# The first two batches' attention output stays in SBUF, and the seven-product stage gets its operands in another order

## The chip, the cores and the metric

The kernel runs on one core of one Trainium2 chip. The metric is device time in microseconds (us) of one execution, the median of several runs; lower is better. All engines work from queues of their own: TensorE (PE, with its weight loads, PEld), VectorE (DVE), ScalarE (ACT), GpSimd (POOL) and SyncE (SP), which here only issues DMAs.

## The reference

Three layers follow one another, in float32. Attention has 4 batches, 12 heads, 448 positions and a head size of 64; it uses a sigmoid in place of a softmax. Its output, 1792 x 768, goes through two feed-forward layers with an inner size of 2048:

```
scores = q @ k.T / 8 - log(448);  attn = sigmoid(scores) @ v      # per batch and head
x  = attn, heads side by side                                     # 1792 x 768
h  = x @ w_in1;   x = (h * sigmoid(h)) @ w_out1                   # first layer
h  = x @ w_in2;   g = (a0 + a1 h + a2 h^2 + a3 h^3) / (1 + |b0||h| + |b1| h^2 + 1e-6)
out = g @ w_out2                                                  # second layer
```

q, k, v are float32; the weights arrive as float64, as bits.

## The kernel before, in words

**Precision.** Most matmuls take operands split into a high part (a ScalarE copy to fp32r) and a low part (a VectorE subtraction of that copy from the source); three passes (high x high, high x low, low x high) make one product. So every operand costs one ScalarE cast and, after it, one VectorE subtraction. `split` does both at once; `split_later` does the cast and leaves the subtraction to the next `flush()`.

**Weights.** `conv()` turns one 128 x 768 piece of float64 weights into float32 by integer work: one ScalarE op (L150), four VectorE ops (L151 to L156), a store to DRAM, and the load of the piece after next. 64 such pieces are spread over the first three stages; what is left when the second matmul of layer 1 begins is spread evenly over its 64 steps.

**Order.** The order on each engine is written out by hand (`tc.manual_schedule()`): it is the order of the calls, and every engine works through its queue in order. Tiles carry the waits; pools opened with `reuse_waits="tile"` may lie where a closed pool lay.

**Stage 1, attention.** 24 head pairs (4 batches x 6), each in two halves, so 48 half steps. A half step multiplies q and k (`attn_QK`, PE L245), applies the sigmoid (ACT L256), transposes a k or q of a later pair (`attn_T`: PE L235 into one spare PSUM bank, read by ACT L237 and then by DVE L238), and multiplies by v (`attn_AV`, PE L263) for the half before. After each pair `attn_E` copies the output from PSUM (DVE L275) and SP stores it to a DRAM tensor xs. A `conv()` stands in every first half up to pair 21.

**Stage 2, first matmul of layer 1**, as seven block products (p1 to p7) in place of eight, for pairs of batches: batches 0 and 1 in groups 0 to 7, batches 2 and 3 in groups 8 to 15. A product is 9 matmuls on PE L416. Its operands are sums and differences of batches (kinds 11, 21, T1 to T4, 22), and sums and differences of weights (s1 to s4 out of one group's `wf` tiles). The order in a group g is p1(g), p2(g), p4(g-1), p6(g), p5(g), p3(g-1), p7(g). `operands0` makes the first set during attention: `load0` reads xs back from DRAM, and one of 21 steps runs in each half from the 26th on. `operands1` and `operands1_late` make the second set during groups 1 to 8, reading xs of batches 2 and 3. `load_w1(g+2)` loads the weights of a group into the `wf` tiles that group g leaves, behind the last read of them (the low part of a22). `sums_12`, `sums_34`, `prep_*` are the weight sums and their splits.

**Stage 3, second matmul of layer 1**, 64 steps `second(n)` of 18 matmuls (PE L552 to L554), each with one operand from DRAM (`load_g`, issued by ACT L518; `split_gd`: ACT L283, DVE L284); in the first 16 steps also a weight piece (`load_wo1`: ACT L533; `split_wo1`: ACT L287, DVE L288). The results p4 and p3 of the last group are worked in between its first steps; `c11` to `c22` apply silu (ACT L435) to the four quarters of a group's result, `keep` and `both` (ACT L490, DVE L305) gather them from PSUM.

**Stage 4, layer 2**, is not touched.

Of the kernel before, what the change touches and what calls it, by code (L numbers as in the profile page):

```python
# [11 lines left out]
F32 = mybir.dt.float32  # L12
F32R = mybir.dt.float32r
# [28 lines left out]
def attention_moe_moe(ctx: ExitStack, tc: tile.TileContext, q, k, v, w_in1, w_out1, w_in2, w_out2, a, b2, out):  # L42
# [23 lines left out]
    def fixed(nm, n, shape, dt, pool=cpool):  # L66
        return [pool.tile(shape, dt, tag=f"{nm}{i}", name=f"{nm}{i}") for i in range(n)]
# [147 lines left out]
    ijH, ijL, s12H, s12L = fixed("wr", 4, [P, DM], F32R, w1_p)  # L215
    s3H, s3L, s4H, s4L, a22H, a22L = fixed("wq", 6, [P, HM], F32R, w1_p)
# [55 lines left out]
    def attn_E(i):  # L272
        b, hp = divmod(i, NP)
        t = xio.get()
# [3 lines left out]
        del vs[i]  # L278
# [51 lines left out]
    sets = ((wf[1][0], wf[1][1], s34f), (wf[0][0], wf[0][1], s12f))  # L330

    def load0(kk):
        x, y, z = (t[:, :S] for t in sets[kk % 2])
        load_b(x, 0, 0, kk, 0)
        load_b(y, 0, 0, kk, 1)
        load_b(z, 0, 1, kk, 1)

    def operands0():
        for kk in range(HK):
            x, y, z = (t[:, :S] for t in sets[kk % 2])  # L340
# [5 lines left out]
            sub(y, z, y)  # L346
            split_b(y, 0, "T3", kk)
            load_b(y, 0, 1, kk, 0)
            yield
            split_b(z, 0, "22", kk)  # L350
            yield
            sub(x, z, x)
            split_b(x, 0, "T2", kk)
            yield
            split_b(y, 0, "21", kk)
            yield
            sub(y, y, x)
            split_b(y, 0, "T4", kk)
            yield
# [3 lines left out]
    def operands1():  # L363
        y, z, y2 = (t[:, :S] for t in xio.free)
        for kk in range(HK):
            x, w = kept["T1", kk], kept["T2", kk]
            load_b(x, 1, 0, kk, 0)
            load_b(y, 1, 0, kk, 1)
            load_b(z, 1, 1, kk, 1)
            load_b(y2, 1, 1, kk, 0)  # L370
            split_b(x, 1, "11", kk)
            yield
            sub(x, y, x)
            split_b(y2, 1, "21", kk)
            yield
            sub(w, z, x)
            yield

    def operands1_late(kind):
        temps = [t[:, :S] for t in xio.free]  # L380
        if kind == "T2":
            for kk in range(HK):
                load_b(temps[kk], 1, 0, kk, 1)
        if kind in ("T2", "T1"):
            for kk in range(HK):
                split_b(kept[kind, kk], 1, kind, kk)
        if kind == "T1":
            for kk in range(HK):
                load_b(kept["T1", kk], 1, 1, kk, 1)
        if kind == "T3":  # L390
            for kk in range(HK):
                sub(temps[kk], kept["T1", kk], temps[kk])
                split_b(temps[kk], 1, kind, kk)
            for kk in range(HK):
                load_b(temps[kk], 1, 1, kk, 0)
        if kind == "22":
            for kk in range(HK):
                split_b(kept["T1", kk], 1, kind, kk)
        if kind == "T4":
            for kk in range(HK):  # L400
                sub(temps[kk], temps[kk], kept["T2", kk])
                split_b(temps[kk], 1, kind, kk)
# [36 lines left out]
    def prep_ij(g):  # L439
        if g < NGR:  # L440
            split_later(wf[g % 2][0], ijH, ijL)
# [7 lines left out]
    def prep_s12(g):  # L449
        if g < NGR:  # L450
            split_later(s12f, s12H, s12L)
# [6 lines left out]
    def prep_s3(g):  # L458
        split_later(s34f[:, :HM], s3H, s3L)

    def prep_s4(g):
        split_later(s34f[:, HM:], s4H, s4L)

    def prep_a22(g):
        split_later(wf[g % 2][1][:, HM:], a22H, a22L)

    def p1(g):
        product(g, "11", bank("a", g), ijH, ijL, 0, True)

    def p2(g):  # L470
        product(g, "21", bank("b", g), ijH, ijL, HM, True)

    def p3(g):
        product(g, "22", bank("c", g), s4H, s4L, 0, False)

    def p4(g):
        product(g, "T4", bank("a", g), a22H, a22L, 0, False)

    def p5(g):
        product(g, "T1", bank("c", g), s12H, s12L, 0, True)  # L480

    def p6(g):
        product(g, "T2", bank("a", g), s12H, s12L, HM, False)

    def p7(g):
        product(g, "T3", bank("a", g), s3H, s3L, 0, False)
# [249 lines left out]
    with tc.manual_schedule():  # L736
# [36 lines left out]
        for i in range(NPT):  # L773
            for h in range(2):
# [21 lines left out]
                if at_half == -6:  # L796
                    load_w1(0)
                flush()
                if i == NPT - 2 and h == 1:
                    prep_ij(0)  # L800
                    sums_12(0)
                if i == NPT - 1:
                    if h == 0:
                        prep_s12(0)
                    else:
                        prep_a22(0)
                if h == 0 and 0 < i < NPT - 2:
                    conv()
# [5 lines left out]
        load_w1(1)  # L814
# [16 lines left out]
        last = NGR - 1  # L831
        for g in range(NGR):
            was = g >= 1
            fill = 1 <= g < HF - 1
# [7 lines left out]
            if g == HF:  # L842
                operands1_late("22")
# [28 lines left out]
            prep_ij(g + 1)  # L872
            if g == HF:
                operands1_late("T4")
# [6 lines left out]
            keep(g, "r")  # L881
            if g:
                prep_a22(g)
            if g == HF - 1:
                operands1_late("T3")
            if fill:
                next(ops1, None)
# [9 lines left out]
            sums_12(g + 1)  # L897
# [21 lines left out]
        c12(last - 1)  # L919
        p4(last)  # L920
# [112 lines left out]
```

## Time and profile before

| | us |
|---|---|
| median of 3 runs (lowest, highest) | 1144.32 (1143.12, 1149.67) |
| the profiled execution | 1145.94 |
| its span, first to last instruction | 1144.2 |
| PE busy in it | 1100.3 (96%) |
| DVE, ACT, POOL busy | 865.0, 633.0, 341.8 |

A wait is listed by the engine that waits, the line of the instruction, and what came last of what it waited for. "xio", "xa", "xb", "wf", "wr", "wq" are tiles, with numbers left out; "km", "qm" are k and q in the order in which they are transposed. PEclk is the granted TensorE clock as a share of full speed.

### The profile page before, as it was taken

To read this page: it belongs to the slowest core of one execution; us is meant where nothing else is said; L and a number is where in the kernel's file an instruction comes from. 1 tells how busy PE (TensorE), PEld (TensorE's weight loads), DVE (VectorE), ACT (ScalarE), POOL (GpSimd) and SP (SyncE) were. 2 spreads that over 40 slices of the span, in tenths; PEclk is the share of its full clock that TensorE was granted. 3 is DMA by queue.
4 is the path that set the end of the run, shared out by engine and by line. 5 is a ranking of instruction groups with operands and counts; after the bars stand their busy time and mean duration, and the time that the engine had idled before them with its cause. 6 is when DMAs were issued, how large, how long until landed. Compare 5 with 4: busy or idle time off the path is not lost.

```text
span 1144.2 us, 15865 instructions
## 1 busy us (share of the span) xinstructions
PE 1100.3 (96%) x5822; PEld 917.0 (80%) x5822; DVE 865.0 (76%) x1028; ACT 633.0 (55%) x1035; POOL 341.8 (30%) x246
## 2 busy tenths in 40 slices
PE   9999989989989979899999899999999999999997
PEld 5554445979889968799999888888999888889997
DVE  4666776758787736866665849789999988788996
ACT  6777767536655534432322436455766665466664
POOL 2111110000000000000000127556677666556774
PEclk9999999989999999999999999999999999999999
DMA  9999975555757757788888655000101010001001
GB/s 254 294 293 309 276 246 178 194 189 185 241 167 230 246 191 235 263 280 289 276 273 294 234 213 222 1 28 15 56 1 47 10 42 1 21 22 56 1 1 42
DMA packets 103805, 183.47 MB, mean 160 GB/s; under 512 B 8752, under 2 KB 77872, under 8 KB 103728
## 3 DMA queue, kind: packets, MB, share of 16 engines
q1 hardware_dynamic: 91504, 160.89, 43.9%
q10 hardware_dynamic: 12160, 21.57, 5.6%
q8 instruction: 46, 0.75, 0.3%
q14 instruction: 31, 0.25, 0.1%
q0 software_dynamic: 64, 0.00, 0.0%
HBM read 126.06 MB, written 56.36 MB: 159 GB/s over the span
## 4 chain that ended last, share of the span: by engine, by line
PE 77%; DMA 9%; DVE 7%; ACT 3%; issue 2%; SPq 1%; ACTq 1%; POOL 0%; DVEq 0%; POOLq 0%
PE acc L683 14%; PE acc L416 9%; PE acc L686 7%; PE hb L614 7%; PE hb L613 7%; PE hb L612 7%; PE hb L263 5%; PE pair L245 4%; PE acc L553 3%; PE acc L554 3%; PE acc L552 3%; PE hb L416 3%; DMA f<-gd 2%; PE hb L235 2%; PE hb L554 1%
## 5 line engine op out<-in xcount | busy, mean ns | idle before, releaser
L288 POOL TENSOR_TENSOR w<-wif,w 128x768 fp32r<-128x768 f32 x33 | 61.7, 1869 | 489.5 <-ACT w L287 484.6
L256 ACT ACTIVATE f<-pair,nls 112x896 f32<-112x896 f32 x96 | 96.7, 1012 | 18.3 <-PE pair L245 18.2
L553 PE MATMUL acc<-xa,woH 128*128 128x448 f32 x252 | 93.2, 370 | 3.1 <-DVE xa L284 3.1
L552 PE MATMUL acc<-xa,woH 128*128 128x448 f32 x252 | 93.0, 369 | 0.0
L554 PE MATMUL acc<-xa,woL 128*128 128x448 f32 x252 | 92.8, 368 | 0.0
L263 PE MATMUL hb<-f,vs 112*64 112x448 f32 x384 | 85.2, 567 | 0.0
L640 DVE RECIPROCAL stg<-stg 128x512 f32<-128x512 f32 (+1 forms) x28 | 84.9, 3032 | 0.0
L627 ACT ACTIVATE stg<-hb,absb 128x512 f32<-128x512 f32 (+1 forms) x44 | 28.0, 636 | 98.0 <-PE hb L614 97.9
L150 ACT ACTIVATE bits<-stg 128x768 f32<-128x768 f32 x64 | 58.0, 906 | 41.7 <-DMA stg<-in_moe_w_in_dram 18.0
L245 PEld LDWEIGHTS pair<-xa,xa 64*112 64x112 f32 x576 | 47.9, 176 | 40.1 <-issue 33.8
L283 ACT CAST xa<-f 128x448 fp32r<-128x448 f32 x64 | 35.9, 563 | 75.8 <-DMA f<-gd 57.2
L245 PE MATMUL pair<-xa,xa 64*112 64x448 f32 x576 | 72.9, 385 | 0.0
L416 PE MATMUL acc<-xb,wr 128*128 128x448 f32 x315 | 69.0, 370 | 0.2 <-ACT f L490 0.2
L288 POOL TENSOR_TENSOR wh<-wif,wh 128x768 fp32r<-128x768 f32 x31 | 57.4, 1851 | 26.7 <-DVE xio L632 23.9
L416 PEld LDWEIGHTS acc<-xb,wr 128*128 128x128 f32 x315 | 60.2, 191 | 6.1 <-issue 0.7
L156 DVE SCALAR_TENSOR_TENSOR bits<-stg,bits 128x768 int32<-128x768 int32 x64 | 63.1, 986 | 2.2
L153 DVE SCALAR_TENSOR_TENSOR bits<-stg,bits 128x768 int32<-128x768 int32 x64 | 62.9, 983 | 2.2
L683 PE MATMUL acc<-w,hx 128*128 128x512 f32 x174 | 61.4, 394 | 0.0
L151 DVE TENSOR_SCALAR bits<-bits 128x768 f32<-128x768 f32 x64 | 36.1, 564 | 32.8 <-ACT bits L150 32.4
L683 PE MATMUL acc<-wh,hx 128*128 128x512 f32 x171 | 60.3, 393 | 0.0
L288 POOL TENSOR_TENSOR w<-wof,w 128x768 fp32r<-128x768 f32 x32 | 59.2, 1849 | 0.4 <-ACT w L287 0.3
L288 POOL TENSOR_TENSOR wh<-wof,wh 128x768 fp32r<-128x768 f32 x32 | 59.2, 1851 | 0.1
(197 smaller groups left out, 3170.6 us busy)
## 6 DMA issues: line engine op xcount, KB each, us to landing
stg<-in_moe_w_in_dram SPq DMA_DIRECT2D x32, 768.0 KB, 6.9
stg<-in_moe_w_out_dram SPq DMA_DIRECT2D x32, 768.0 KB, 5.6
gd<-f SPq DMA_DIRECT2D x64, 224.0 KB, 3.3
f<-gd ACTq DMA_DIRECT2D x64, 224.0 KB, 4.6
wf<-w0i SPq DMA_DIRECT2D x32, 384.0 KB, 5.9
w0i<-bits SPq DMA_DIRECT2D x16, 384.0 KB, 4.1
w0o<-bits SPq DMA_DIRECT2D x16, 384.0 KB, 2.6
wos<-w0o ACTq DMA_DIRECT2D x16, 384.0 KB, 4.7
```

The source lines that it names most:

```text
L245: nc.tensor.matmul(p[:CP, j, :S], K[rows[j], a_, c * CP : (c + 1) * CP], Q[rows[j], b_, :], start=(n == 0), stop=(n == 2),)
L256: nc.scalar.activation(t[:CP], p[:CP, :, :S], AF.Sigmoid, bias=nls[:CP], scale=QKSCALE)
L263: nc.tensor.matmul(pav[0][j * D : (j + 1) * D, :S], vs[i][:, j, c * D : (c + 1) * D], t[:CP, j], start=(c == 0), stop=(c == NCH - 1),)
L288: (eng or nc.vector).tensor_tensor(out=lo, in0=src, in1=h.bitcast(F32), op=ALU.subtract)
L416: nc.tensor.matmul(o, w_[:, w], x[:, i_, :], start=first and kk == 0 and n_ == 0, stop=kk == HK - 1 and n_ == 2, skip_group_check=not first,)
L552: nc.tensor.matmul(o, woH[c][:, w], x[:, 0, :], start=(c == 0), stop=False)
L553: nc.tensor.matmul(o, woH[c][:, w], x[:, 1, :], start=False, stop=False)
L554: nc.tensor.matmul(o, woL[c][:, w], x[:, 0, :], start=False, stop=(c == KF - 1))
L612: nc.tensor.matmul(o, wh[:, w], x[:, 0, :wd_], start=first, stop=False)
L613: nc.tensor.matmul(o, wh[:, w], x[:, 1, :wd_], start=False, stop=False)
L640: nc.vector.reciprocal(t0, t1)
L683: nc.tensor.matmul(acc[t][:, :BK], a_, w_[:, :BK], start=first, stop=last)
```

## The change

Four things are changed. (1) `attn_E` leaves the output of batches 0 and 1 in twelve SBUF tiles `xk`, stores nothing to DRAM for them, and `operands0` works on these tiles; its steps start four halves earlier, and each subtraction now stands behind the split of the step, for the next step to use. The `xk` tiles lie where the split weights `wr`, `wq` lie later. (2) The last `conv()` in attention is that of pair 18, `load_w1(0)` and `load_w1(1)` come eight halves before the end, the first weight splits from five halves before the end. (3) In stage 2 `operands1` issues its loads a step or more before it splits them; T3 and T4 are subtracted for all three tiles some products before they are split; `sums_12` moves from behind p3 to behind p4, `prep_s3` from behind p4 to behind p6, `prep_ij` from behind p6 to behind p5; a `conv()` stands in groups 0, 2, 4, 6 and 10 to 15 (before: 9 to 15). (4) At the end of stage 2 the last group's c21, the gathering of its r and c12 move behind the third step of stage 3. The order on PE and on POOL is the same as before.

```
+    xk = fixed("xk", 2 * KD, [P, S], F32, xk_p)
     def attn_E(i):
+        if b < 2:
+            nc.vector.tensor_copy(xk[b * KD + hp], pav[0][:, :S])
+            return
     def operands0():
         for kk in range(HK):
-            x, y, z = (t[:, :S] for t in sets[kk % 2])
+            x, w, y, z = (xk[kk + n_ * HK] for n_ in range(4))
             split_b(x, 0, "11", kk)
+            sub(x, y, x)
             yield
-            sub(x, y, x)
             split_b(x, 0, "T1", kk)
+            sub(y, z, y)
             yield
...
     def operands1():
+        load(0)
+        yield
         for kk in range(HK):
-            load_b(x, 1, 0, kk, 0)
...
             split_b(x, 1, "11", kk)
             yield
+            split_b(y2, 1, "21", kk)
             sub(x, y, x)
-            split_b(y2, 1, "21", kk)
             yield
             sub(w, z, x)
+            if kk + 1 < HK:
+                load(kk + 1)
+                yield
             yield
...
-                if at_half >= -NOPS - 2:
+                if at_half >= -NOPS - 6:
                     next(first_ops, None)
-                for kk, when in enumerate((-NOPS - 5, -NOPS - 4, -NOPS + 6 + 1)):
-                    if at_half == when:
-                        load0(kk)
...
-                if h == 0 and 0 < i < NPT - 2:
+                if h == 0 and 0 < i < NPT - 5:
                     conv()
...
             both(g, "s1", "b")
-            prep_s3(g)
-            if g == HF - 1:
-                operands1_late("T1")
-            if fill:
-                next(ops1, None)
-            if g in (0, 2, 4, 6) or g > HF:
+            sums_12(g + 1)
+            if was:
+                fill(g)
+            if g in (0, 2, 4, 6) or g > HF + 1:
                 conv()
...
         p4(last)
-        both(last, "u3", "c")
         c22(last)
         second(1)
-        c21(last)
         p3(last)
-        both(last, "r", "c")
-        c12(last)
...
             second(n)
+            if n == 2:
+                c21(last)
+                both(last, "r", "c")
+                c12(last)
```

VectorE in attention, one head pair (pair 15; hb0 is the spare bank, hb1 the output; xa are split k and q, xb the operands). Before:

```order
L238 TENSOR_TENSOR xa4_220<-hb0_276,xa4_220 128x448
L302 TENSOR_TENSOR wf1_1_252<-wf1_1_252,wf1_0_251 128x448
L284 TENSOR_TENSOR xb6_234<-wf1_1_252,xb6_234 128x448
L238 TENSOR_TENSOR xa5_221<-hb0_276,xa5_221 128x448
L275 COPY xio0_61<-hb1_277 128x448
L284 TENSOR_TENSOR xb1_229<-wf0_0_249,xb1_229 128x448
L151 TENSOR_SCALAR bits0_66<-bits0_66 128x768
L152 TENSOR_SCALAR bits0_66<-bits0_66 128x768
L153 SCALAR_TENSOR_TENSOR bits0_66<-stg1_65,bits0_66 128x768
L156 SCALAR_TENSOR_TENSOR bits0_66<-stg1_65,bits0_66 128x768
L238 TENSOR_TENSOR xa0_216<-hb0_276,xa0_216 128x448
```

and in the changed kernel, the densest kind of pair:

```order
L239 TENSOR_TENSOR xa2_218<-hb0_281,xa2_218 128x448
L288 TENSOR_TENSOR xb13_241<-xk1_259,xb13_241 128x448
L306 TENSOR_TENSOR xk7_265<-xk10_268,xk7_265 128x448
L239 TENSOR_TENSOR xa3_219<-hb0_281,xa3_219 128x448
L280 COPY xio2_63<-hb1_282 128x448
L288 TENSOR_TENSOR xa7_223<-xk7_265,xa7_223 128x448
L306 TENSOR_TENSOR xk7_265<-xk10_268,xk1_259 128x448
L151 TENSOR_SCALAR bits2_68<-bits2_68 128x768
L152 TENSOR_SCALAR bits2_68<-bits2_68 128x768
L153 SCALAR_TENSOR_TENSOR bits2_68<-stg0_64,bits2_68 128x768
L156 SCALAR_TENSOR_TENSOR bits2_68<-stg0_64,bits2_68 128x768
L239 TENSOR_TENSOR xa4_220<-hb0_281,xa4_220 128x448
```

The subtraction (L302, now L306) has moved behind the split that it stood ahead of.

VectorE in group 0 of stage 2, from the weight sums s3, s4 (sf1) to the low part of s3 (wq1). Before:

```order
L302 TENSOR_TENSOR sf1_254<-wf0_0_249,wf0_1_250 128x384
L302 TENSOR_TENSOR sf1_254<-wf0_0_249,sf0_253 128x384
L305 TENSOR_TENSOR f_60<-acc2_1994,f_60 128x448
L151 TENSOR_SCALAR bits0_66<-bits0_66 128x768
L152 TENSOR_SCALAR bits0_66<-bits0_66 128x768
L153 SCALAR_TENSOR_TENSOR bits0_66<-stg1_65,bits0_66 128x768
L156 SCALAR_TENSOR_TENSOR bits0_66<-stg1_65,bits0_66 128x768
L298 TENSOR_TENSOR wq1_260<-sf1_254,wq0_259 128x384
```

and in the changed kernel:

```order
L306 TENSOR_TENSOR sf1_254<-wf0_0_249,wf0_1_250 128x384
L306 TENSOR_TENSOR sf1_254<-wf0_0_249,sf0_253 128x384
L309 TENSOR_TENSOR f_60<-acc2_1968,f_60 128x448
L309 TENSOR_TENSOR sf0_253<-wf1_1_252 128x384
L306 TENSOR_TENSOR sf0_253<-sf0_253,wf1_0_251 128x384
L151 TENSOR_SCALAR bits0_66<-bits0_66 128x768
L152 TENSOR_SCALAR bits0_66<-bits0_66 128x768
L153 SCALAR_TENSOR_TENSOR bits0_66<-stg0_64,bits0_66 128x768
L156 SCALAR_TENSOR_TENSOR bits0_66<-stg0_64,bits0_66 128x768
L302 TENSOR_TENSOR wq1_1844<-sf1_254,wq0_1843 128x384
```

The two sums of the next group (sf0 out of wf1) now stand ahead of the conversion and of wq1.

ScalarE at the change from stage 2 to stage 3 (acc0 is the last group's result, gd the DRAM operands, woH the split weights). Before:

```order
L435 ACTIVATE f_60<-f_60 128x448 x2
L435 ACTIVATE f_60<-acc0_1992 128x448
L435 ACTIVATE f_60<-f_60 128x448
L287 CAST woH2_3693<-wos2_3497 128x768
L533 DMA wos2_3497<-w0o6_158 128x768
L283 CAST xa2_218<-f_60 128x448
L518 DMA f_60<-gd4_0_97 128x448
L283 CAST xa3_219<-f_60 128x448
```

and in the changed kernel:

```order
L442 ACTIVATE f_60<-f_60 128x448 x2
L291 CAST woH2_3656<-wos2_3464 128x768
L540 DMA wos2_3464<-w0o6_158 128x768
L287 CAST xa2_218<-f_60 128x448
L525 DMA f_60<-gd4_0_97 128x448
L442 ACTIVATE f_60<-acc0_1966 128x448
L442 ACTIVATE f_60<-f_60 128x448
L287 CAST xa3_219<-f_60 128x448
```

The two silus of the last group now stand behind the operands of step 2 and ahead of those of step 3.

## Rows read from the trace of the kernel before

**Rows 1.** Windows, two stages: us, busy of PE, PEld, DVE, ACT, POOL; PEclk; DMA share, GB/s.

```profile
88.40:195.10 106.70, 95.17 (x606) 47.11 (x605) 77.55 (x117) 79.09 (x109) 15.00 (x20) 0.97 0.82 253
195.10:409.90 214.80, 205.05 (x991) 187.81 (x991) 159.65 (x265) 118.92 (x219) 0.00 (x0) 0.98 0.64 212
```

**Rows 2.** Waits of PE: line, releaser, us in total, times, longest.

```profile
PE hb L235 <- DVE xa L238: 11.5, 8, 2.1
PE acc L416 <- ACT f L490: 8.5, 3, 5.4
...
PE hb L416 <- ACT f L490: 1.0, 1, 1.0
PE acc L416 <- DVE wq L298: 0.3, 1, 0.3
```

**Rows 3.** Chain of waits, attention and stage 2: start, us, what.

```profile
12.82 1.66 PE hb L263 x8
...
88.42 1.68 PE hb L263 x8
...
182.74 1.65 PE hb L263 x8
...
228.22 6.67 DMA T<-xs
...
239.51 8.51 PE acc L416 x27
...
273.82 12.77 PE acc L416 x63
```

**Rows 4.** Timeline of DVE, attention without operand steps: start, us, what.

```profile
69.13 0.56 DVE L151 TENSOR_SCALAR bits<-bits 128x768 f32<-128x768 f32 x1
...
72.19 0.61 DVE L238 TENSOR_TENSOR xa<-hb,xa 128x448 fp32r<-128x448 f32 x1
```

**Rows 5.** Timeline of PE, the transpose that follows.

```profile
73.42 0.60 PE L235 MATMUL hb<-ident,qm 112*128 112x112 f32 x4
```

**Rows 6.** Timeline of DVE, attention with operand steps.

```profile
107.13 0.93 DVE L151 TENSOR_SCALAR bits<-bits 128x768 f32<-128x768 f32 x1 [0.19 <-ACT bits L150]
...
139.54 0.61 DVE L275 COPY xio<-hb 128x448 f32<-128x448 f32 x1
140.07 0.61 DVE L302 TENSOR_TENSOR wf<-sf,wf 128x448 f32<-128x448 f32 x1
```

**Rows 7.** Timeline of POOL, its copy at the first of these.

```profile
107.03 0.61 POOL L193 COPY km<-ks 112x512 f32<-112x512 f32 x1 [9.05 <-DMA ks<-in_k_dram]
```

**Rows 8.** Timeline of ACT, the last of the three T4 casts in stage 2.

```profile
317.54 0.56 ACT L283 CAST xb<-xio 128x448 fp32r<-128x448 f32 x1 [1.23 <-DVE xio L302]
```

**Rows 9.** Timeline of DVE, stage 2: a low part, a weight sum.

```profile
203.11 0.95 DVE L298 TENSOR_TENSOR wr<-wf,wr 128x768 fp32r<-128x768 f32 x1
203.98 0.55 DVE L305 TENSOR_TENSOR sf<-wf 128x384 f32<-128x384 f32 x1
```

**Rows 10.** Tile wf, groups 10 to 15: landing of its loads.

```profile
DMA to landing us min/median/max: 5.9/6.5/7.7
```

**Rows 11.** Timeline of DVE, stage 3: low parts of three weight pieces.

```profile
452.85 0.96 DVE L288 TENSOR_TENSOR woL<-wos,woH 128x768 fp32r<-128x768 f32 x1
...
458.73 0.95 DVE L288 TENSOR_TENSOR woL<-wos,woH 128x768 fp32r<-128x768 f32 x1
...
461.96 0.96 DVE L288 TENSOR_TENSOR woL<-wos,woH 128x768 fp32r<-128x768 f32 x1
```

**Rows 12.** Timeline of ACT, the operand of step 3.

```profile
428.85 0.56 ACT L283 CAST xa<-f 128x448 fp32r<-128x448 f32 x1
```

**Rows 13.** Timeline of PE, first matmuls of step 2.

```profile
428.98 0.47 PE L552 MATMUL hb<-xa,woH 128*128 128x448 f32 x1 [4.00 <-ACT xa L283]
...
430.34 0.57 PE L552 MATMUL hb<-xa,woH 128*128 128x448 f32 x1
430.71 0.57 PE L553 MATMUL hb<-xa,woH 128*128 128x448 f32 x1
```

More of the change, by code (lines that the diff above doesn't have):

```diff
@@ L328, in split_b @@
         split(src, x)
-    sets = ((wf[1][0], wf[1][1], s34f), (wf[0][0], wf[0][1], s12f))
-    def load0(kk):
-        x, y, z = (t[:, :S] for t in sets[kk % 2])
-        load_b(x, 0, 0, kk, 0)
-        load_b(y, 0, 0, kk, 1)
-        load_b(z, 0, 1, kk, 1)
     def operands0():
         for kk in range(HK):
-            x, y, z = (t[:, :S] for t in sets[kk % 2])
+            x, w, y, z = (xk[kk + n_ * HK] for n_ in range(4))
             split_b(x, 0, "11", kk)
+            sub(x, y, x)
             yield
-            sub(x, y, x)
             split_b(x, 0, "T1", kk)
+            sub(y, z, y)
             yield
-            sub(y, z, y)
             split_b(y, 0, "T3", kk)
-            load_b(y, 0, 1, kk, 0)
+            sub(y, z, x)
             yield
@@ L364, in operands1, with load @@
         y, z, y2 = (t[:, :S] for t in xio.free)
-        for kk in range(HK):
-            x, w = kept["T1", kk], kept["T2", kk]
-            load_b(x, 1, 0, kk, 0)
+        def load(kk):
+            load_b(kept["T1", kk], 1, 0, kk, 0)
             load_b(y, 1, 0, kk, 1)
@@ L370, in operands1 @@
             load_b(y2, 1, 1, kk, 0)
+        load(0)
+        yield
+        for kk in range(HK):
+            x, w = kept["T1", kk], kept["T2", kk]
             split_b(x, 1, "11", kk)
             yield
+            split_b(y2, 1, "21", kk)
             sub(x, y, x)
-            split_b(y2, 1, "21", kk)
             yield
             sub(w, z, x)
+            if kk + 1 < HK:
+                load(kk + 1)
+                yield
             yield
@@ L389, in operands1_late @@
                 load_b(kept["T1", kk], 1, 1, kk, 1)
+        if kind == "T3 sums":
+            for kk in range(HK):
+                sub(temps[kk], kept["T1", kk], temps[kk])
         if kind == "T3":
             for kk in range(HK):
-                sub(temps[kk], kept["T1", kk], temps[kk])
                 split_b(temps[kk], 1, kind, kk)
@@ L398, in operands1_late @@
                 split_b(kept["T1", kk], 1, kind, kk)
+        if kind == "T4 sums":
+            for kk in range(HK):
+                sub(temps[kk], temps[kk], kept["T2", kk])
         if kind == "T4":
             for kk in range(HK):
-                sub(temps[kk], temps[kk], kept["T2", kk])
                 split_b(temps[kk], 1, kind, kk)
@@ L450, in prep_s12 @@
         if g < NGR:
-            split_later(s12f, s12H, s12L)
+            split_later(s12f, wr[2], wr[3])
     def sums_34(g):
@@ L790, in attention_moe_moe @@
                 at_half = 2 * i + h - 2 * NPT
-                if at_half >= -NOPS - 2:
+                if at_half >= -NOPS - 6:
                     next(first_ops, None)
-                for kk, when in enumerate((-NOPS - 5, -NOPS - 4, -NOPS + 6 + 1)):
-                    if at_half == when:
-                        load0(kk)
-                if at_half == -6:
+                flush()
+                if at_half == -8:
                     load_w1(0)
-                flush()
-                if i == NPT - 2 and h == 1:
+                    load_w1(1)
+                if at_half == -5:
+                    xk_s.close()
+                    wr_p, wr_s = opened("wr")
+                    wr.extend(fixed("wr", 4, [P, DM], F32R, wr_p))
+                    wq.extend(fixed("wq", 6, [P, HM], F32R, wr_p))
                     prep_ij(0)
                     sums_12(0)
[L802 to L806, printed above, removed]
-                if h == 0 and 0 < i < NPT - 2:
+                if at_half == -3:
+                    prep_s12(0)
+                if at_half == -1:
+                    prep_a22(0)
+                if h == 0 and 0 < i < NPT - 5:
                     conv()
@@ L831, in attention_moe_moe, with fill @@
         last = NGR - 1
+        def fill(g):
+            if g < HF - 1:
+                next(ops1, None)
         for g in range(NGR):
             was = g >= 1
-            fill = 1 <= g < HF - 1
             p1(g)
@@ L842, in attention_moe_moe @@
             if g == HF:
+                operands1_late("T3")
+            if g == HF + 1:
                 operands1_late("22")
@@ L871, in attention_moe_moe @@
                 c21(g - 1)
-            prep_ij(g + 1)
+            prep_s3(g)
+            if g == HF - 1:
+                operands1_late("T1")
             if g == HF:
-                operands1_late("T4")
+                operands1_late("T4 sums")
             if g == last:
@@ L881, in attention_moe_moe @@
             keep(g, "r")
+            prep_ij(g + 1)
             if g:
                 prep_a22(g)
[L884 to L887, printed above, removed]
+            fill(g)
+            if g == HF:
+                operands1_late("T4")
             if g == last:
@@ L896, in attention_moe_moe @@
             load_w1(g + 2)
-            sums_12(g + 1)
+            if g == HF - 1:
+                operands1_late("T3 sums")
             if g == last - 1:
@@ L919, in attention_moe_moe @@
         c12(last - 1)
+        both(last, "u3", "c")
         p4(last)
-        both(last, "u3", "c")
         c22(last)
         second(1)
-        c21(last)
         p3(last)
-        both(last, "r", "c")
-        c12(last)
+        wr_s.close()
         w1_s.close()
```

38 lines of the change are left out of this document (18 added, 20 removed).

## The prediction

> **What bounds the kernel now.** I read the windows by stage first: the reader is to see that PE is busy for 95.17 of the 106.70 us of the later attention and 205.05 of the 214.80 us of stage 2 [rows 1]. PE bounds the kernel, so only time that PE stands still, or runs at its lower clock, can be won. The waits of PE come second: 11.5 us for DVE's reading of the transposed q and k, in eight waits, and 8.5 + 1.0 + 0.3 us in stage 2, most of it for one ScalarE copy out of PSUM that is late [rows 2]. The chain of waits comes third and tells how much is lost in all.
>
> In attention the half steps come every 3.60 us up to 88.42 ((88.42 - 12.82) / 21 steps); the next 22 steps should take 79.2 us and take 94.3 [rows 3]. So 15.1 us are lost there: the 11.5 us of waits, and 3.6 us behind them, in part at a lower clock. The loss begins where the operand steps do. DVE shows why, by its order: a period holds the copy of the output, two splits, one or two subtractions, a conversion and two readings of the transposes, and a split whose source was only just subtracted waits for ACT's cast in between.
>
> In stage 2 the longest wait of PE, 5.4 us, ends at 239.51. Ahead of it the chain shows a load of xs of 6.67 us [rows 3]: ACT, in order, stands at the cast of a tile whose load was only just issued, and the copy that PE waits for is queued behind. Then 27 matmuls take 8.51 us, where 63 undisturbed ones take 12.77, or 0.203 each [rows 3]: 8.51 - 5.47 = 3.0 us more, at the lower clock. The other waits, 8.5 - 5.4 + 1.0 = 4.1 us, stand at groups 7 and 8, where a cast waits 1.23 us for the subtraction ahead of it [rows 8], three times in T3 and three times in T4, with a copy for PE queued behind. So stage 2 loses 5.4 + 3.0 + 4.1 + 0.3 = 12.8 us.
>
> **Attention.** Twelve stores and twelve loads leave SP's queue, and with them 5.5 MB. SP no longer holds q, k, v loads behind loads that wait for stores. Nothing is added to DVE: the copy goes to another tile, splits and subtractions are as many as before. What moves is their order, so the waits for casts go. What is late next is DVE itself. Without operand steps its reading of a transposed k ends at 72.19 + 0.61 = 72.80, and PE takes up the spare bank at 73.42 [rows 4, 5]: 0.62 us to spare. In the first half of a pair a split and, in most, a subtraction now stand between the output copy and the conversion, 0.53 us each (139.54 to 140.07) [rows 6]. A split alone fits; with a subtraction it is 1.06 - 0.62 = 0.44 us too late. Eight pairs (11 to 18) have both operand steps and a conversion, and by the order five of them the subtraction: 2.2 us. POOL adds to it: while its copy of k ran at 107.03, a conversion op took 0.93 us in place of 0.56 [rows 4, 6, 7], 0.37 more. Once in each of the five pairs that are late is 1.9 us. I take 4.0 us lost, so 11.1 won. The bounds: nothing lost (15.1 won), and in all eight pairs the 0.44 and two such collisions, 8 x 1.18 = 9.4 lost (5.7 won).
>
> The Trainium skill ("SBUF — State Buffer", section "SBUF: two separate sides") says that DVE and GpSimd share a port pair as an exclusive lock, held for a whole instruction, and that a DVE op with two SBUF inputs takes it too. That speaks against this change, which packs such subtractions where POOL's copies fall. The 0.93 us agrees that the two get in each other's way; by the rule a collision would cost up to one whole POOL copy, 0.61 us.
>
> The three conversions that leave (3.06 us of DVE each, 69.13 to 72.19 [rows 4]) stood in pairs 19 to 21; those pairs then have DVE to spare. The four early weight loads and first splits stand behind the last operand step; the `xk` tiles that the splits overwrite have been read by then, so I cost this at nothing.
>
> **Stage 2.** With a load issued half a group (6 us) or more ahead of its cast, against 6.67 us for the slowest shown, the 5.4 us and the 3.0 at low clock go; the second and third loads have a whole group, 12.8 us. With the three subtractions ahead of all three casts the 4.1 us go. SP may now wait for a subtraction before such a load, with stores and the load of a conversion behind it, and none of these is needed within a group.
>
> Two costs come. In group 0 PE waited 0.3 us at p7 for the low part of s3, which stands behind a conversion; now two sums, 0.55 us each [rows 9], stand ahead of it too: 0.3 + 1.1 = 1.4 us. And `sums_12` now stands three products earlier, 5.5 us, while the load it reads is still issued behind the low part of a22. From that low part round to the next one: the load 6.5 us [rows 10], two sums 1.1, a conversion 3.06, the low parts of s3, ij and a22, 0.55 + 0.87 + 0.55 (203.11 to 203.98 for the long one [rows 9]), together 12.6 us, against 12.77 for a group. It just fits; at 7.7 us it is 1.1 us late per group with a conversion. I take 0.5 us in all, bounds 0 and 6 x 1.1 = 6.6 (groups 10 to 15). So stage 2 wins 12.8 - 1.4 - 0.5 = 10.9 us, bounds 4.8 and 11.4.
>
> **Stage 3.** Before, step 2's operands stood behind c12, which waits for the last p3: PE waited 4.00 us, from 424.98 to 428.98, and about ten matmuls ran at 0.37 us each instead of 0.203 [rows 13], 1.7 us more. These 5.7 us go at that point. But I expect them back. From step 3 on, a chain through ACT and DVE sets the pace: a step without a conversion takes 461.96 - 458.73 = 3.2 us, one with it 458.73 - 452.85 = 5.9 [rows 11], against 18 x 0.203 = 3.65 on PE. Step 3's cast stood at 428.85, 3.9 us behind p3's end [rows 12, 13]; now it stands behind both and c12, and so begins 0.6 + 0.5 us behind it, 2.8 earlier. PE comes 5.7 earlier. And as 36 conversions are left in place of 32, eight and not seven fall into steps 3 to 15: 5.9 - 3.2 = 2.7 us more. Won: 2.8 - 2.7 = 0.1 us; bounds -5 (the load latencies of this stretch once more) and +5.7. One cast of s3 now stands just ahead of the operands of step 0: 0.4 us lost. The other conversions lie beside steps where PE had no lasting wait: nothing, with the bound of -5 covering it.
>
> **Sum.** 11.1 + 10.9 + 0.1 - 0.4 = 21.7 us. The profiled execution took 1145.94, so 1124.2; the median of the runs lies 1.6 us below it, so 1122.6.
>
> **Rivals.**
> - *DVE stays the bound of attention.* 5.7 won there in place of 11.1: 1128.0. For it: DVE is as full as before. Against it: the waits for casts, which were part of each period, go. Chance 0.17. By the Trainium skill's rule on the shared pair ("SBUF — State Buffer"), as an estimate, 0.61 us for each of two copies in each of eight pairs, 9.8 us, would bring the time out here too.
> - *Conversion pace.* The four conversions that moved into stage 3 take 2.7 us each from PE, one in the sum already: 8.1 more, 1130.7. For it: the chain of rows 11; against it: from step 16 on no weight pieces stand in the chain. Chance 0.15.
> - *The sums meet their loads* (slower). In the ten groups with a conversion DVE waits for the load at `sums_12`, and p7 and p1 wait for low parts behind it. It decides from 21.7 / 10 + 6.6 = 8.8 us of landing on; at 9.5 us it costs 10 x 2.9 = 29 us: 1151.6. Against it: the slowest shown is 7.7. Chance 0.04.
> - *The change does not do what it says*: the stalls only move to the next load or cast, and just one of the two stages gains, some 11 us: 1133. Chance 0.07.
> - *Better*: no collisions, and stage 3 keeps its 5.7: 15.1 + 11.4 + 5.7 - 0.4 = 31.8 won, 1112.5. Nothing in DVE's order excludes it. Chance 0.10.
>
> The forecast itself has 0.47; its own range is 1117 to 1128. The range for 8 in 10 is 1112 to 1133. Half a per cent, 5.7 us, is about what a measurement of this kernel can tell from no change: faster than that 0.93, within it 0.03, slower 0.04.
>
> **What would show it.** Right: attention ends near 184 (before: 195.1), the waits of PE for DVE's reading of the transposes fall to some 3 us in few pieces; no wait over 2 us in stage 2, one of about 1.4 at the first p7, and no stretch of 0.37 us matmuls there; stage 2 lasts about 204; step 2 of stage 3 follows p3 at once, and more waits for low parts of weights come in steps 5 to 15. Wrong: DVE waiting at `sums_12` for a load in group after group, or PE still waiting two microseconds at every transposition of q.

## The result, and the profile after

The changed kernel takes 1132.43 us (median of 4 runs, 1128.91 to 1134.14), the kernel before 1145.09 beside it: ratio 0.988, 95% interval 0.984 to 0.992. The forecast was 1122.6 with a range of 1112 to 1133, so the time lies just inside the range and 10 us above its centre. The profiled execution took 1133.58 us, against 1145.94 before: 12.4 us won.

Windows of the changed kernel: later attention, stage 2, and stage 3 from step 2 to step 63 (columns as in [rows 1], which answer to the first two).

```profile
87.96:182.39 94.43, 91.74 (x605) 46.20 (x605) 66.59 (x104) 77.54 (x105) 14.16 (x19) 1.00 0.73 222
182.39:387.13 204.74, 201.95 (x992) 185.31 (x991) 154.28 (x259) 119.43 (x218) 0.00 (x0) 1.00 0.63 212
403.12:654.97 251.85, 234.12 (x1100) 207.54 (x1099) 167.31 (x234) 81.93 (x128) 4.61 (x2) 0.99 0.79 261
```

The kernel before, steps 2 to 63:

```profile
428.98:667.36 238.38, 230.75 (x1098) 206.98 (x1099) 155.82 (x218) 78.12 (x123) 4.33 (x2) 0.99 0.77 257
```

The reader is to see two things. Attention ends at 182.39 in place of 195.10, and stage 2 takes 204.74 in place of 214.80: at step 0 of stage 3 the change is 409.90 - 387.13 = 22.8 us ahead. But steps 2 to 63 take 13.5 us more than before, with PE standing 251.85 - 234.12 = 17.7 us there in place of 7.6. (DVE works 11.5 us more: four conversions.) The lead by step: 25.9 us at step 2, 22.2 at step 16, 19.7 at steps 32 and 48, 12.4 at step 63, and nothing changes after that.

The waits of PE in the changed kernel (columns as in [rows 2]):

```profile
PE acc L560 <- DVE xa L288: 6.1, 8, 2.4
PE hb L560 <- DVE xa L288: 4.7, 5, 1.3
PE acc L559 <- ACT xa L287: 3.5, 1, 3.5
PE hb L559 <- DVE f L309: 2.8, 1, 2.8
PE hb L236 <- DVE xa L239: 2.7, 5, 0.6
PE hb L561 <- DVE woL L292: 1.9, 5, 0.4
PE hb L559 <- ACT woH L291: 1.7, 1, 1.7
PE acc L423 <- DVE wq L302: 1.5, 2, 1.3
...
PE hb L423 <- DVE wq L302: 1.3, 1, 1.3
```

Of [rows 2], the 11.5 us for transposes are 2.7 us in five pieces, and the 8.5 us for ScalarE's copy are gone. What stands at the top now are operands and weight pieces of stage 3 (L559 to L561). In stage 2 two waits of 1.3 remain, and DVE's timeline there shows, at the sums that groups 11 to 14 make for the next group, what answers to [rows 9, 10]:

```profile
327.53 0.56 DVE L309 TENSOR_TENSOR sf<-wf 128x384 f32<-128x384 f32 x1 [2.09 <-DMA wf<-w0i]
...
340.72 0.56 DVE L309 TENSOR_TENSOR sf<-wf 128x384 f32<-128x384 f32 x1 [2.40 <-DMA wf<-w0i]
...
355.05 0.56 DVE L309 TENSOR_TENSOR sf<-wf 128x384 f32<-128x384 f32 x1 [3.54 <-DMA wf<-w0i]
...
368.11 0.56 DVE L309 TENSOR_TENSOR sf<-wf 128x384 f32<-128x384 f32 x1 [2.26 <-DMA wf<-w0i]
```

The sums do meet their loads, but of each 2 to 3.5 us only the longest reaches PE (1.30 at 359.78).

The timeline of ACT, around steps 50 to 55, is the place of the longest wait in stage 3:

```profile
602.45 0.55 ACT L287 CAST xa<-f 128x448 fp32r<-128x448 f32 x1
607.48 0.91 ACT L150 ACTIVATE bits<-stg 128x768 f32<-128x768 f32 x1 [4.48 <-DMA wif<-w1i]
613.96 0.62 ACT L603 CAST hx<-xio 128x512 fp32r<-128x512 f32 x1 [5.58 <-DMA xio<-xs]
613.97 0.34 ACTq L525 DMA_DIRECT2D f<-gd  x1
614.49 0.56 ACT L287 CAST xa<-f 128x448 fp32r<-128x448 f32 x1
```

Between 602.45 and 614.49 ACT casts no operand for PE: it stands at a conversion and at the cast of layer 2's x, and PE waits 3.53 us at 615.10. Before the change ACT had lead enough to hide such stands (the account below gives it at step 48).

### The profile page after: what moved, and what is told of

It is laid out like the page before. It is cut to its first block, busy times and chain, and to the rows that moved or that the text cites. A ratio compares the mean times of both kernels' runs of the same rounds, so it can differ in the third digit from the quotient of the medians.

```text
span 1131.8 us, 15809 instructions
## 1 busy us (share of the span) xinstructions
PE 1096.3 (97%) x5822; PEld 913.8 (81%) x5822; DVE 862.2 (76%) x1028; ACT 636.3 (56%) x1035; POOL 341.8 (30%) x246
## 4 chain that ended last, share of the span: by engine, by line
PE 80%; DVE 8%; DMA 7%; ACT 2%; issue 2%; ACTq 1%; SPq 0%; POOL 0%; DVEq 0%; POOLq 0%
PE acc L690 14%; PE acc L423 10%; PE acc L693 7%; PE hb L621 7%; PE hb L619 7%; PE hb L620 7%; PE hb L264 6%; PE pair L246 5%; PE hb L423 4%; PE acc L560 3%; PE acc L561 3%; PE acc L559 3%; DMA f<-gd 3%; PE hb L236 2%; DVE bits L153 1%
## 5 line engine op out<-in xcount | busy, mean ns | idle before, releaser
L559 PE MATMUL acc<-xa,woH 128*128 128x448 f32 x252 | 93.9, 372 | 3.6 <-ACT xa L287 3.5
L561 PE MATMUL acc<-xa,woL 128*128 128x448 f32 x252 | 93.4, 371 | 0.0
L264 PE MATMUL hb<-f,vs 112*64 112x448 f32 x384 | 82.5, 551 | 0.0
L423 PE MATMUL acc<-xb,wr 128*128 128x448 f32 x315 | 67.8, 366 | 0.0
L423 PEld LDWEIGHTS acc<-xb,wr 128*128 128x128 f32 x315 | 59.0, 188 | 5.5 <-issue 0.7
L288 DVE TENSOR_TENSOR xa<-f,xa 128x448 fp32r<-128x448 f32 x64 | 39.0, 620 | 30.1 <-ACT xa L287 30.1
```

The source lines that it names most:

```text
L264: nc.tensor.matmul(pav[0][j * D : (j + 1) * D, :S], vs[i][:, j, c * D : (c + 1) * D], t[:CP, j], start=(c == 0), stop=(c == NCH - 1),)
L423: nc.tensor.matmul(o, w_[:, w], x[:, i_, :], start=first and kk == 0 and n_ == 0, stop=kk == HK - 1 and n_ == 2, skip_group_check=not first,)
L559: nc.tensor.matmul(o, woH[c][:, w], x[:, 0, :], start=(c == 0), stop=False)
L561: nc.tensor.matmul(o, woL[c][:, w], x[:, 0, :], start=False, stop=(c == KF - 1))
```

## The experiments

**e1: conversions put back.** The four that moved into stage 3 go back to attention (three) and stage 2 (one).

```
-                if h == 0 and 0 < i < NPT - 5:
+                if h == 0 and 0 < i < NPT - 2:
-            if g in (0, 2, 4, 6) or g > HF + 1:
+            if g in (0, 2, 4, 6) or g > HF:
```

> The changed kernel with the four conversions put back where they were (pairs 19 to 21 of attention, group 9 of stage 2), so that 32 and not 36 are left for stage 3. Theory 'conversion pace' (the four extra conversions set the pace of stage 3 and cost about 10 us there): steps 2 to 63 of stage 3, which take 238.4 us in the kernel before and 251.9 in the changed one, take 238 to 243; attention and stage 2 lose 0 to 2 us; the whole is 1120 to 1125. Rival 'latency' (stage 3 got slower because its loads and stores now fall otherwise, whatever the number of conversions): steps 2 to 63 still take 249 to 253 and the whole is 1131 to 1135.

Measured: 1124.01 us, ratio 0.981 (0.979 to 0.983). Steps 2 to 63, windows:

```profile
408.76:645.87 237.11, 228.24 (x1100) 207.20 (x1099) 155.54 (x218) 78.62 (x124) 3.96 (x2) 0.99 0.77 257
```

So with the four, stage 3 takes 251.85 - 237.11 = 14.7 us more. Some 2 us of this are another thing, a slower pace of PE's matmuls in the changed kernel (see e7): 28 of its 61 steps lasted 3.72 us, and none of e1's, where an undisturbed step lasts 3.65. Step 0 comes 5.5 us later than in the changed kernel (attention 1.8, the rest in stage 2), where 0 to 2 were expected. That is no clean price of the old places: in e6, which is the changed kernel up to there, step 0 comes 3.9 us later too, and e8 and e10, which differ in the four alone, have it within 0.8 us of each other.

**e2: the kernel before, with 36 conversions in stage 3.** The same two lines, changed the other way in the kernel before.

```
-                if h == 0 and 0 < i < NPT - 2:
+                if h == 0 and 0 < i < NPT - 5:
-            if g in (0, 2, 4, 6) or g > HF:
+            if g in (0, 2, 4, 6) or g > HF + 1:
```

> The kernel before with only the four conversions moved to stage 3 (none in pairs 19 to 21 and group 9). 'Conversion pace': steps 2 to 63 of stage 3 take 246 to 252 us in place of 238.4; attention ends some 3 to 5 us earlier, since its last pairs carry no conversion; the whole is 1147 to 1155. Rival 'latency': steps 2 to 63 take 237 to 241 and the whole is 1139 to 1143.

Measured: 1152.32 us, ratio 1.005 (1.003 to 1.007): half a per cent slower. Steps 2 to 63 took 245.5, 7.1 more than before, although here only 18 steps lasted 3.72 us, against 44 before; attention ended 2.8 earlier. The price is there without the rest of the change.

**e3: c12 ahead of step 2 again.**

```
         second(1)
+        c21(last)
         p3(last)
+        both(last, "r", "c")
+        c12(last)
         wr_s.close()
...
-            if n == 2:
-                c21(last)
-                both(last, "r", "c")
-                c12(last)
```

> The changed kernel with c21, the gathering of r and c12 of the last group put back ahead of step 2's operands. If the weight pieces' chain sets the pace of steps 2 to 15 (as predicted), step 2 begins 4 to 6 us later behind p3, but step 16 at the same time within 2 us, and the whole is 1131 to 1135. Rival: the wait removed was a gain that lasts: step 16 and the end are 4 to 6 us later, 1137 to 1139.

Measured: 1133.96 us, ratio 0.989 (0.987 to 0.991). The timeline of PE has the wait of [rows 13] again:

```profile
406.58 0.47 PE L559 MATMUL hb<-xa,woH 128*128 128x448 f32 x1 [4.00 <-ACT xa L287]
```

The time is that of the changed kernel within its spread. Counted from the end of the last p3, step 3 begins 9.8 us behind it here and 3.5 in the changed kernel, step 16 66.4 and 63.8 (64.3 before). So of 6.3 us that the removed wait and the slow matmuls behind it save at step 3, 3.7 are given back by step 16 and 2.6 are left: nearer the theory (the same within 2 us) than its rival (4 to 6 later), and near the 2.8 that the prediction had left there before it took off the eighth conversion. By step 63 1.3 are left, but the changed kernel had 22 more steps at the slower pace, 1.5 us.

**e4: subtraction before the split, output still in SBUF.** All operand steps in their old order; the first two are shown.

```
             split_b(x, 0, "11", kk)
-            sub(x, y, x)
             yield
-            split_b(x, 0, "T1", kk)
-            sub(y, z, y)
+            sub(x, y, x)
+            split_b(x, 0, "T1", kk)
             yield
...
```

> The changed kernel with each subtraction of the first operand set put back ahead of the split in the same step; the output still stays in SBUF, with no stores or loads. Theory 'order' (ACT's cast waits for DVE's subtraction, and DVE for the cast): PE's waits for DVE's reading of the transposes rise from 2.7 to 6 to 11 us, attention ends at 187 to 194 in place of 182.4, the whole is 1136 to 1143. Rival 'trips through DRAM' (the loads of xs in SP's queue and their stores were what held attention up): waits under 4 us, attention ends at 182 to 184, the whole is 1131 to 1135.

Measured: 1142.57 us, ratio 0.997 (0.995 to 0.998). PE's waits:

```profile
PE hb L236 <- DVE xa L239: 10.4, 7, 2.3
```

Attention ends at 195.0: all 12.7 us are lost again, although no operand goes through DRAM. This refutes that the way through DRAM alone made attention slow.

**e5: x loads of layer 2 five steps earlier.**

```
+            if m == -4:
+                for d in range(HK):
+                    load_x(0, d)
             if m == 1:
...
-                for d in range(HK):
-                    load_x(0, d)
```

> The changed kernel, with the first three loads of the second layer's x issued at step 44 in place of step 49 (they read batches 0 and 1, stored long before). The open point: steps 48 to 63 of stage 3 take 66.4 us in the changed kernel and 59.0 in the one before. Theory A (ACT in order): at 608.4 ACT stands 5.58 us at the cast of such a load, which SP issued only at 604.6, behind a store and four weight loads; the loads for step 51 stand behind it in ACT's queue and PE waits 3.5 us. Then that wait of 5.58 goes, steps 48 to 63 take 61 to 63.5 us, and the whole 1127 to 1130. Theory B (the transfers themselves are too many there; the DMA engines are 0.73 busy from step 48 to 63 and near full from 588 to 612): the wait only moves to the loads of gd or of a conversion; steps 48 to 63 stay at 65 to 67, the whole at 1131 to 1134.

Measured: 1129.2 us, ratio 0.986 (0.980 to 0.992); steps 48 to 63 took 61.3 us in place of 66.4. Theory A holds: 5 us of the 7.3 lost there come from ACT standing at a load that SP issued late.

**e6: weight loads of stage 3 one step later.**

```
         split_wo1(2)
-        load_wo1(6)
...
             load_g(n + 2)
+            load_wo1(n + 4)
             second(n)
...
                 split_wo1(n + 1)
-                load_wo1(n + 5)
```

> The changed kernel, with each load of a weight piece for the first layer's second product issued one step later (at the start of the next step), so that ACT no longer stands, at its own issue of the load, for DVE's reading of the tile that it fills. Theory (ACT standing at its issue is part of the chain that sets the pace of steps 2 to 15): its waits for DVE's woL there (17 us in 7 in the changed kernel) fall under 6, steps 2 to 16 take 61 to 62.5 us in place of 63.95, the whole 1129 to 1131.5. Rival (the pace is set by the conversions and by the loads of gd, so that ACT waits there instead): steps 2 to 16 take 63.5 to 65 us, the whole 1131.5 to 1134; a wait of PE for woH or woL of over 1 us would show that the loads now come too late.

Measured: 1122.15 us (1119.36 to 1128.79), ratio 0.980 (0.974 to 0.986). Steps 2 to 16, in windows of this kernel and then of the changed one:

```profile
407.76:464.33 56.57, 54.20 (x253) 48.49 (x252) 45.33 (x62) 25.83 (x39) 0.00 (x0) 0.97 0.82 275
```

```profile
403.12:467.07 63.95, 55.88 (x253) 48.06 (x252) 45.61 (x62) 25.83 (x39) 0.00 (x0) 0.97 0.72 240
```

The same work, 7.4 us sooner, more than the 1.5 to 3 that I expected: the direction was right, the size not. In this stretch ACT stood at its own issue of a load until DVE had read the tile. (These waits fell from 17.0 to 9.1 us, not under 6 as expected.)

**e7: sums_12 back behind p3.**

```
-            sums_12(g + 1)
             if was:
                 fill(g)
...
                 p3(g - 1)
             flush()
+            sums_12(g + 1)
```

> The changed kernel, with the two sums for s12 put back from the place behind p4 to the place behind p3, as it was before the change. Theory (the sums meet their loads, at a small size): DVE's waits at the sums for the w1 load, 2.1 to 3.5 us in four groups, go, and with them the waits of PE at p7 (1.31 at group 0, 1.30 at 359.78) and 0.15; step 0 starts 1.5 to 2.8 us earlier against attention's end, the whole 1129.5 to 1131. Rival (they cost nothing that counts, and the sums' old place is what made PE wait at group boundaries before): the low parts of s12 or ij come late again, waits of 0.3 to 1 us in several groups, the whole 1132 to 1135.

Measured: 1126.49 us, ratio 0.983 (0.978 to 0.988). PE's waits at L423:

```profile
PE acc L423 <- DVE wq L302: 0.3, 1, 0.3
```

2.8 us of waits became 0.3, yet stage 2 lasted 205.07 and not less: here its matmuls ran at a slower pace. The chain of this kernel, and of the changed one:

```profile
215.64 13.02 PE acc L423 x63
```

```profile
215.27 12.77 PE acc L423 x63
```

Over 16 groups that is 4.0 us, which hid the gain in the profiled run. The waits bear out the theory; the rest of the gain in time (5.9 us in all) lies in stage 3, which this edit does not touch, so its size is not settled.

**e9: gd loads three steps ahead.**

```
+            if n == 2:
+                load_g(4)
-            load_g(n + 2)
+            load_g(n + 3)
```

> The changed kernel, with the loads of the second product's input (gd) in stage 3 issued three steps ahead in place of two. Theory A (chain of gd loads): ACT waits 65.9 us in 26 pieces for these loads from step 2 to 63; a load lands 4.4 to 6 us after its issue, and its cast holds up the issue of the next ones, so the casts fall behind PE where conversions add to them. Then these waits fall under 25 us, steps 2 to 63 take 243 to 248 us in place of 251.85, the whole 1124 to 1129. Theory B (the conversions' own round sets the pace: load into one of two tiles, ACT, DVE, then the next load, some 5.5 us each): ACT's waits move to the conversions' loads (38.7 us now, then over 70), steps 2 to 63 take 250 to 253, the whole 1131 to 1134.

Measured: 1128.47 us (1126.23 to 1133.51), ratio 0.985 (0.980 to 0.991). ACT's waits from step 2 to 63 in this kernel, and in the changed one:

```profile
ACT bits L150 <- DMA stg<-in_moe_w_in_dram: 53.4, 9, 6.7
...
ACT xa L287 <- DMA f<-gd: 9.0, 6, 3.4
```

```profile
ACT xa L287 <- DMA f<-gd: 65.9, 26, 5.4
ACT bits L150 <- DMA stg<-in_moe_w_in_dram: 38.7, 9, 6.2
```

The waits for gd nearly go, those for the next piece to convert grow, and steps 2 to 63 take 251.1 us as before: theory B, by the profile. The median is 4 us better, as A said, but the profiled run shows none of it; on time this run is inconclusive.

**e8: e1, e5, e6 and e7 together.** The diff is those four, the first of them

```
+                if h == 0 and 0 < i < NPT - 2:
+            if g in (0, 2, 4, 6) or g > HF:
...
```

> Four edits of the earlier runs together, on the changed kernel: the four conversions back in attention and stage 2, the sums for s12 back behind p3, the weight loads of stage 3 a step later, the loads of the second layer's x at step 44. Theory (each removes a stand of its own, so that gains add up apart from the overlap in stage 3): stage 2 loses under 1.5 us to waits for wq, steps 2 to 63 take 228 to 234 us (62 steps... 61 steps of 3.65 to 3.72 are 222.7 to 226.9), the whole 1114 to 1120. Rival (the conversions alone set stage 3's pace and the other edits only shift waits about): steps 2 to 63 stay at 236 to 239 as with the conversions alone put back, the whole 1120 to 1124.

Measured: 1105.9 us (1103.22 to 1112.06, 6 runs), ratio 0.965 (0.963 to 0.968), better than either theory and the best version found. Steps 2 to 63:

```profile
402.30:627.63 225.33, 223.46 (x1099) 205.91 (x1098) 154.91 (x218) 78.61 (x124) 4.25 (x2) 1.00 0.80 271
```

PE stands 1.9 us in 61 steps, against a floor of 61 x 3.65 = 222.7.

**e10: the same without the conversions put back,** so as the change has them:

```
                 if h == 0 and 0 < i < NPT - 5:
             if g in (0, 2, 4, 6) or g > HF + 1:
```

> The same without the conversions put back: the changed kernel with the sums behind p3, the weight loads a step later and the x loads at step 44, so 36 conversions in stage 3. Theory (the four conversions cost 7.9 us in stage 3 mainly through ACT's stands, which steps 2 to 16 lost when the weight loads went a step later): steps 2 to 63 take 233 to 238 us, step 0 comes 2 to 5 us earlier than in the kernel with the conversions back, the whole 1115 to 1121, within 3 us of that one. Rival (each of the four costs PE about 2 us whatever else is mended): steps 2 to 63 take over 238, the whole is 4 to 8 us above that of the kernel with the conversions back.

Measured: 1120.45 us, ratio 0.978 (0.975 to 0.980). Steps 2 to 63:

```profile
401.75:641.80 240.05, 230.82 (x1100) 206.69 (x1098) 167.28 (x234) 82.11 (x128) 4.10 (x2) 0.99 0.82 274
```

The rival won, and by more than it said: with the four conversions these steps take 240.05 - 225.33 = 14.7 us more here too, as between e1 and the changed kernel. Of the steps here 44 lasted 3.72 us, and in e8 2 lasted 3.70 or 3.72 and 56 lasted 3.65; that accounts for 42 x 0.07 = 2.9 of it, and some 11.8 us, or 2.9 each, are stalls and what follows them.

**e11: kept tile stored and loaded back at once.** This and the next one ask whether the order alone suffices.

```
+            nc.sync.dma_start(out=xs[0][hp][:, b * S : (b + 1) * S], in_=x)
+            nc.sync.dma_start(out=x, in_=xs[0][hp][:, b * S : (b + 1) * S])
```

> The changed kernel, with each of the twelve outputs of the first two batches stored to DRAM and loaded back into the same tile, so that its transfers are those of the kernel before (24 more in SP's queue, 5.5 MB) while the order of splits and subtractions stays that of the change. Theory (what was won in attention came from the order; the way through DRAM cost little): attention ends at 182 to 185.5 us, the whole within 3 us of the changed kernel, 1129 to 1136. Rival (SP standing at such a load for its store holds up loads of q, k and v behind it): waits of PE for the transposes come back, attention ends at 187 or later, the whole 1137 or more.

Measured: 1180.22 us, ratio 1.030 (1.027 to 1.032). The rival, by far: attention ends at 234.06. The queue of SP, then the waits of PE:

```profile
SPq L280 <- DMA xs<-xk: 82.8, 12, 8.4
```

```profile
PE hb L236 <- DVE xa L239: 29.4, 12, 6.9
```

Twelve loads, each directly behind the store that it reads, hold SP for 82.8 us, with the loads of q, k and v behind them.

**e12: loaded back two pairs later.** The same, with the load issued in `attn_E(i)` for pair i - 2.

```
+        if 0 <= i - 2 < 2 * NP:
+            b2, hp2 = divmod(i - 2, NP)
+            nc.sync.dma_start(out=xk[b2 * KD + hp2], in_=xs[0][hp2][:, b2 * S : (b2 + 1) * S])
...
+            nc.sync.dma_start(out=xs[0][hp][:, b * S : (b + 1) * S], in_=x)
```

> The changed kernel with the twelve outputs stored to DRAM and loaded back into their tiles two pairs (14.4 us) after the store, as the kernel before had its loads well behind its stores: the same 24 transfers and 5.5 MB more, but SP stands at no store. Theory (in the run before this one attention ended at 234 because SP stood 82.8 us in twelve waits for its own stores; the transfers as such cost little): attention ends at 182 to 186, SP's waits for xs fall under 5 us, the whole 1130 to 1136. Rival (the bytes themselves cost: 5.5 MB at some 280 GB/s are 20 us of transfer, and loads of q, k, v land later): waits of PE for the transposes of 5 us or more come back, attention ends at 187 to 195, the whole 1136 to 1145.

Measured: 1145.71 us, ratio 1.000 (0.998 to 1.001): just past the rival's 1145, and attention ended at 197.55, past its 195. ACT, at the split of pair 9's output, and then PE:

```profile
110.57 0.56 ACT L292 CAST xb<-xk 128x448 fp32r<-128x448 f32 x1 [10.02 <-DMA xk<-xs]
```

```profile
112.88 1.46 PE L246 MATMUL pair<-xa,xa 64*112 64x448 f32 x6 [7.76 <-ACT f L257]
```

DVE had written pair 9's output by 85.1; a subtraction reads it at 93.28 (here still the first copy), and ACT wants to split it from 100.5 on. The load, issued two pairs later (102.55), took 8.0 us (its median here, as for the stores), and the sigmoid queued behind the cast held PE for 7.76 us. The waits for transposes rose from 2.7 to 6.8 as well. My placing of the load caused the one long stall, so this run does not price the bytes; it shows how little time the new order leaves for a way through DRAM: 8 to 15 us, where a store and a load take 8 each.

## Why the prediction was right or wrong

**Attention: right.** 12.7 us won against 11.1. The five late pairs are there, 0.46 to 0.60 us each, near the 0.44 worked out. What was too high was the 1.9 for collisions of DVE and POOL: from 87.96 to 182.39 three operations of DVE are lengthened, by 1.0 us together, and where DVE has room. One such is DVE's subtraction of 0.92 us at 95.50, others taking 0.62, between two of POOL's copies:

```profile
95.50 0.92 DVE L306 TENSOR_TENSOR xk<-xk,xk 128x448 f32<-128x448 f32 x1
```

```profile
95.13 0.81 POOL L193 COPY km<-ks 112x512 f32<-112x512 f32 x1 [6.07 <-DMA ks<-in_k_dram]
95.89 1.00 POOL L193 COPY qm<-qs 112x512 f32<-112x512 f32 x1
```

The rival that DVE bounds attention fell with it. The Trainium skill ("SBUF — State Buffer", section "SBUF: two separate sides") has a DVE instruction with two SBUF inputs and a GpSimd instruction that reads SBUF exclude each other for a whole instruction. The trace agrees: the subtraction ends at 96.42, 0.48 us behind the end of the first copy (95.94), and the second copy at 96.89, 0.47 us behind the subtraction. What was wrong in my estimate of 9.8 us was the count: I had sixteen such collisions hold DVE for 0.61 us each, and three did, for 0.26 to 0.41; others lengthened a copy of POOL, for which PE did not wait in this stretch.

My reason was half the cause. By e4 the order of subtraction and split is needed, as I said. By e11 and e12 the order does not suffice either, where outputs go through DRAM: it asks for them about as soon as they can come back. In the forms tried, neither alone wins anything; a load placed between those of e11 and e12 was not tried.

**Stage 2: right.** 10.1 us won against 10.9 - 0.4. The first p7 waits 1.31 us (1.4 forecast). The sums meet their loads in four groups, and PE pays 1.3 + 0.2 us for it, against 0.5 forecast. With e7 2.5 of these 2.8 us go.

**Stage 3: wrong, and this is the miss.** Forecast +0.1, measured 22.8 - 12.4 = 10.4 us lost. The step that failed is "The other conversions lie beside steps where PE had no lasting wait: nothing, with the bound of -5 covering it." I priced one of four conversions, at 2.7 us, and took the steps of the others for free because PE did not wait there. PE did not wait because ACT and DVE were ahead, and the conversions eat that lead. DVE's low part for step 48 and the first matmul of that step, in the kernel before:

```profile
597.41 0.62 DVE L284 TENSOR_TENSOR xa<-f,xa 128x448 fp32r<-128x448 f32 x1
```

```profile
608.33 0.37 PE L552 MATMUL acc<-xa,w 128*128 128x448 f32 x1
```

and in the changed kernel:

```profile
585.33 0.62 DVE L288 TENSOR_TENSOR xa<-f,xa 128x448 fp32r<-128x448 f32 x1
```

```profile
588.59 0.37 PE L559 MATMUL acc<-xa,w 128*128 128x448 f32 x1
```

The lead there is 10.9 us before and 3.3 after the change, and 9.5 again in e1; the last 7.3 us are lost right behind it, in steps 48 to 63. Four at 2.7 are 10.8 us; e1, e2 and e10 give 14.7, 7.1 and 14.7, and at one pace of PE's matmuls some 12.8, 9.0 and 11.8 (28, 26 and 42 steps at 0.07 us taken off, added and taken off). So the price of a piece was about right, 2.2 to 3.2 us, and what failed was to charge it once and not four times. This was my rival "conversion pace" with its chance of 0.15; its 1130.7 lies 1.7 us from the 1132.4. (The rival at 1133, that the change does not do what it says, lies nearer by number, but both stages gained, so it is not what happened.) What spoke against mine, "from step 16 on no weight pieces stand in the chain", was true and beside the point: from there on the operand loads, the next pieces and, from step 49, the x loads of layer 2 take their place in ACT's queue (e5, e9). What sets the price of a piece there, its load, the DMA engines (0.79 busy) or its place in ACT's order, none of these runs separates.

That the whole still ended inside 1112 to 1133 is luck as far as stage 3 goes: the range was wide, and attention came out 1.6 us better. The 10.4 us lost lie outside the bounds of -5 and +5.7 of its term, and 1132.4 lies outside the 1117 to 1128 that the forecast gave for itself.

Up to step 16 the forecast of this stage held. The lead is 22.8 us at step 0 and 22.2 at step 16, so 9.8 of the 10.4 us are lost behind it. The give-back of the wait at step 2 was forecast as 2.9 of 5.7 us, with 2.8 left; by e3 it was 3.7 of 6.3, with 2.6 left. The eighth conversion in these steps was to take 2.7: step 16 stands 63.8 us behind the last p3 in the changed kernel and 61.3 in e1, which has seven there.

## What to carry to other kernels

An engine that works ahead in a queue of its own hides stalls only until its lead is spent: price work added beside a "never waiting" engine at the full time of the chain it joins, every piece and not the first alone. Look in such a queue for casts that stand at a load just issued, and for DMA issues that wait until their tile is read: moving these, with e7, was worth 1132.43 - 1120.45 = 12.0 us, as much as the change itself. Keeping data on chip and reordering its use were worth nothing apart, in the forms tried, and 12.7 us together.

## What the runs showed of the hardware

The same fp32r matmuls of 128 x 448 run at one of two paces, 0.2027 or 0.2067 us apart (12.77 or 13.02 us for 63 matmuls; 3.65 or 3.72 for a step of 18), at a granted clock of 1.00 in either. A pace can hold for long: the changed kernel had the faster one throughout stage 2, and e7, e8 and e10 the slower for 196.9 us on end; e8 then had the faster in nearly all of stage 3. Many of the changes come at a stall of PE, but not all: in e5 it goes from the slower to the faster at 374.05, with no stall of PE from 207.1 to 388.4. It is worth 4.0 us in stage 2 and 4.4 in stage 3, as much as some of these edits, and probably part of why runs of one kernel spread by 5 us or more. What sets it stays open; none of the runs was made to tell.
